# Attention over 128 heads on one core: unrolled instruction streams rewritten as loops with register addresses on four engines

## The chip, the cores and the metric

The kernel runs on one core of one Trainium2 chip. The metric is the device time of one execution in microseconds (us). A profile of one execution shows every instruction of the engines TensorE (PE, and PEld for its weight loads), VectorE (DVE), ScalarE (ACT), GpSimd (POOL) and SyncE (SP), and the DMA traffic.

## The reference

```python
B, H, Sq, Skv, Dh = 8, 16, 16, 2048, 256          # bfloat16
scale = q.shape[-1] ** -0.5
scores = jnp.einsum('bhqd,bhkd->bhqk', q, k) * scale
attn = softmax(scores, axis=-1)
return jnp.einsum('bhqk,bhkd->bhqd', attn, v)
```

There are 128 heads. Each has 16 queries, 2048 keys and 2048 values of 256 numbers. K and V are 128 MB each (2^27 bytes), read once; the queries and the output are 1 MB each.

## The kernel before, in words

The 128 heads are worked in 16 blocks of 8 heads (`G = 16`). The K of a block is two units of 4 MB, `e = 0` and `e = 1` (below: a and b), and so is its V. A unit fills one of four slots of the SBUF tensor `SL` (128 partitions x 64 rows `t` x 256 numbers, 32 KB in each partition). Two slots (`KA`, `KB`) take K and two (`VA`, `VB`) take V; block 0's K goes through the V slots and the last block's V through the K slots.

For block `g` the work is:

- SP issues all loads of K and V (line 97, in `on_sync`), each behind a wait for the work that frees its slot. The order is K a, K b of block g, then V a, V b of block g-1. The last V units are split into pieces (`TAIL_A`, `TAIL`) so that TensorE can follow them as they land. The queries come with one load into `QT` (line 100).
- VectorE turns each K unit in place with 32x32 block transposes, four instructions of 16 rows `t` for a unit (line 154).
- TensorE computes the scores into `S_ps` with 64 matmuls of 512 columns (lines 234 and 235, called by `qk`). The stationary operand is `QW`, in which ScalarE lays out the scaled queries of the block (`qwb`, line 174).
- VectorE takes the negated maximum of the scores (line 156), ScalarE the exponentials and their sums (line 206), VectorE transposes these into `PTc` (line 162) and forms the reciprocal of the sum (lines 164, 166), and ScalarE spreads `PTc` into the zero-padded stationary operand `PTz` with eight copies (line 219).
- TensorE multiplies `PTz` with V, 64 matmuls of 256 columns for a unit (line 251, `pv`), unit a into one PSUM bank and unit b into another. ScalarE scales each half of the rows into `O_fin` (`evac`, line 180) and issues the store of the block (line 184). The last block's store is issued by SP (line 133).

TensorE's blocks 1 to 15 are one loop (`nc.Fori`), with blocks 0 and the last product written out around it; the other engines' programs are fully written out. In TensorE's loop the scores of block g come first and then the product with V of block g-1. On ScalarE, block g-1's `finish` (evacuation and store) stands between block g's exponentials and block g's copies into `PTz`.

The semaphores that matter here: `s_k`, `s_v` count landed loads, `c_kt` transposed K, `c_qk` finished scores of a unit, `c_mx` the maximum, `c_ex` the exponentials, `c_pt` the transposes into `PTc`, `c_cp` the copies into `PTz`, `c_pv` finished products, `c_ev` evacuations.

Of the kernel before, what the change touches and what calls it, by code (L numbers as in the profile page):

```python
# [7 lines left out]
PE = mybir.EngineType.PE  # L8
BF16 = mybir.dt.bfloat16
F32 = mybir.dt.float32  # L10

T = 64
KA, KB, VA, VB = 0, 1, 2, 3


def bass_standalone__softmax_full_bidir__sampling_kernel(
# [17 lines left out]
    qh = q.rearrange("b h s d -> (b h) (s d)")  # L34
    oh = out.rearrange("b h s d -> (b h s) d")

    with ExitStack() as es:
# [5 lines left out]
        PTc = ec(nc.sbuf_tensor("PTc", [128, T, 32], BF16))  # L43
        PTz = ec(nc.sbuf_tensor("PTz", [128, 2, T, 128], BF16))
        O_fin = ec(nc.sbuf_tensor("O_fin", [128, 2, D], BF16))
        negm = ec(nc.sbuf_tensor("negm", [128, G], F32))
        lsum = ec(nc.sbuf_tensor("lsum", [128, G, 2], F32))
        ltot = ec(nc.sbuf_tensor("ltot", [128, G], F32))
        rinv = ec(nc.sbuf_tensor("rinv", [128, G], F32))

        S_ps = ec(nc.psum_tensor("S_ps", [128, 4, 512], F32))
        O_ps = ec(nc.psum_tensor("O_ps", [128, 4, 512], F32))
# [4 lines left out]
        s_q = sem("s_q")  # L57
        s_k = [sem("s_ka"), sem("s_kb")]
        s_k0 = [sem("s_k0a"), sem("s_k0b")]
        s_v = [sem("s_va"), sem("s_vb")]  # L60
        s_st = [sem("s_st%d" % i) for i in range(2)]
# [4 lines left out]
        c_kt = [[sem("c_kt%d%d" % (e, h)) for h in range(2)] for e in range(2)]  # L66
        c_qk = [sem("c_qka"), sem("c_qkb")]
# [5 lines left out]
        c_pv = [sem("c_pv0"), sem("c_pv1")]  # L73
        c_pl = sem("c_pl")
# [4 lines left out]
        def ap_of(t_ap, offset, dims):  # L79
            return bass.AP(tensor=t_ap.tensor, offset=offset, ap=[list(t_ap.ap[0])] + [list(d) for d in dims])  # L80


        TAIL = [(0, 19), (19, 14), (33, 10), (43, 7), (50, 5), (55, 4), (59, 3), (62, 2)]
        TAIL_A = [(0, 37), (37, 27)]
        s_tail = [sem("s_t%d" % i) for i in range(len(TAIL))]
        s_vl = [sem("s_vl%d" % i) for i in range(len(TAIL_A))]
        s_vc = sem("s_vc")
        s_kl = sem("s_kl")

        def obank(g, e):  # L90
            return e + (2 if g == last else 0)

        def kslot(g, e):
            return (VA, VB)[e] if g == 0 else (KA, KB)[e]
# [4 lines left out]
        def on_sync(eng):  # L99
            eng.dma_start(QT[:], qh).then_inc(s_q, 16)  # L100
            for e in range(2):
                load(eng, ku, 0, e, kslot(0, e), 0, T, s_k0[e])
            for g in range(1, G):
                for e in range(2):
                    if g >= 2:
                        eng.wait_ge(c_qk[e], g)
                    if (g, e) != (last, 1):
                        load(eng, ku, g, e, kslot(g, e), 0, T, s_k[e])
                    else:
                        load(eng, ku, g, e, kslot(g, e), 0, 32, s_k[e])  # L110
                        load(eng, ku, g, e, kslot(g, e), 32, 32, s_kl)
                w = g - 1
                for e in range(2):
                    if w:
                        eng.wait_ge(c_pv[e], w)
                    else:
                        eng.wait_ge(c_qk[e], 1)
                    if (w, e) != (last - 1, 1):
                        load(eng, vu, w, e, (VA, VB)[e], 0, T, s_v[e])
                        if e:  # L120
                            eng.sem_inc(s_vc, 16)
                    else:
                        load(eng, vu, w, e, VB, 0, 32, s_v[e])
                        load(eng, vu, w, e, VB, 32, 32, s_vc)

            eng.wait_ge(c_qk[0], G)
            for (a, n), s in zip(TAIL_A, s_vl):
                load(eng, vu, last, 0, KA, a, n, s)
            eng.wait_ge(c_qk[1], G)
            for (a, n), s in zip(TAIL, s_tail):  # L130
                load(eng, vu, last, 1, KB, a, n, s)
            eng.wait_ge(c_ev, 2 * last + 2)
            eng.dma_start(oh[128 * last:128 * last + 128, :], O_fin[:, last % 2, :]).then_inc(s_fin, 16)
            eng.wait_ge(s_fin, 16)

        def on_gpsimd(eng):
            eng.memset(PTz[:].rearrange("p a t c -> p (a t c)").bitcast(F32), 0.0).then_inc(c_pool, 1)  # L137

        def on_vector(eng):
            eng.memset(QW[:].rearrange("p e m x -> p (e m x)").bitcast(F32), 0.0).then_inc(c_qt, 1)  # L140
            eng.wait_ge(s_q, 16)
            qf = QT[:].bitcast(F32)
            eng.transpose(qf, qf).then_inc(c_qt, 1)  # L143
            for g in range(G):
                for e in range(2):
                    for c in range(4):
                        if g == 0 and c == 0:
                            eng.wait_ge(s_k0[e], 16)
                        elif c == 0:
                            eng.wait_ge(s_k[e], 16 * g)  # L150
                        elif (g, e, c) == (last, 1, 2):
                            eng.wait_ge(s_kl, 16)
                        x = SLf[:, kslot(g, e), 16 * c:16 * c + 16, :].rearrange("p t i -> p (t i)")
                        eng.transpose(x, x).then_inc(c_kt[e][c // 2], 1)  # L154
                eng.wait_ge(c_qk[1], g + 1)
                eng.tensor_reduce(out=negm[:, g:g + 1], in_=S_ps[:].rearrange("p c n -> p (c n)"),  # L156
                                  axis=AX.X, op=ALU.max, negate=True).then_inc(c_mx, 1)
                for h in range(2):
                    eng.wait_ge(c_ex[h], g + 1)
                    if g and h == 0:  # L160
                        eng.wait_ge(c_cp, 8 * g)
                    eng.transpose(PTc[:, 32 * h:32 * h + 32, :].rearrange("p t x -> p (t x)"),  # L162
                                  P_sb[:, 1024 * h:1024 * h + 1024]).then_inc(c_pt, 1)
                eng.tensor_reduce(out=ltot[:, g:g + 1], in_=lsum[:, g, :], axis=AX.X, op=ALU.add).then_inc(c_ri, 1)  # L164
                eng.wait_ge(c_ri, 2 * g + 1)
                eng.reciprocal(rinv[:, g:g + 1], ltot[:, g:g + 1]).then_inc(c_ri, 1)  # L166

        def on_scalar(eng):
            def qwb(g):
                Q, r = g // 4, g % 4  # L170
                for a in range(4):
                    dv = QW[32 * a:32 * a + 32, 0, 16 * a, :]
                    sv = QT[32 * Q:32 * Q + 32, :]
                    eng.activation(ap_of(dv, dv.offset, [[1024 + 512, 2], [2, 64], [1, 2]]),  # L174
                                   ap_of(sv, sv.offset + 2 * (8 * r + a), [[8, 2], [64, 64], [1, 2]]),
                                   ACTF.Copy, scale=scale).then_inc(c_qw, 1)

            def evac(g, e):
                rows = slice(64 * e, 64 * e + 64)
                eng.activation(O_fin[rows, g % 2, :], O_ps[rows, obank(g, e), 0:D],  # L180
                               ACTF.Copy, scale=rinv[rows, g:g + 1]).then_inc(c_ev, 1)

            def store(g):
                eng.dma_start(oh[128 * g:128 * g + 128, :], O_fin[:, g % 2, :]).then_inc(s_st[g % 2], 16)

            def finish(g):
                eng.wait_ge(c_ri, 2 * g + 2)
                if g >= 2:
                    eng.wait_ge(s_st[g % 2], 16 * (g // 2))
                for e in range(2):  # L190
                    eng.wait_ge(c_pv[e], g + 1)
                    evac(g, e)
                eng.wait_ge(c_ev, 2 * g + 2)
                store(g)
# [3 lines left out]
            for g in range(G):  # L198
                if g < last:
                    eng.wait_ge(c_qk[1], g + 1)  # L200
                    qwb(g + 1)
                eng.wait_ge(c_mx, g + 1)
                if g:
                    eng.wait_ge(c_pt, 2 * g)
                for h in range(2):
                    eng.activation(P_sb[:, 1024 * h:1024 * h + 1024],  # L206
                                   S_ps[:, 2 * h:2 * h + 2, :].rearrange("p c n -> p (c n)"), ACTF.Exp,
                                   bias=negm[:, g:g + 1], scale=1.0, accum_out=lsum[:, g, h:h + 1]).then_inc(c_ex[h], 1)
                if 0 < g < last:
                    finish(g - 1)  # L210
                if g == 0:
                    eng.wait_ge(c_pool, 1)
                eng.wait_ge(c_pt, 2 * g + 2)
# [104 lines left out]
```

## Time and profile before

| | |
|---|---|
| time, 3 runs | median 636.15 us, 636.04 to 636.17 |
| the profiled execution's own time | 636.1 us |
| its span, first to last instruction | 634.8 us |
| busy: PE / DVE / ACT / POOL | 77% / 58% / 34% / 1% of the span |
| granted TensorE clock, mean | 0.917 |
| moved by DMA | 270.64 MB, mean 426 GB/s |

The span is 1.3 us shorter than the time of the same execution. A row of the profile's timeline gives the start and the duration in us, then the engine, the line, the operation and what it writes and reads, then how many instructions it merges; in brackets stands how long the engine was idle before and what ended that. A row of DMA issues gives the number of loads, the KB of one, and the median us from issue to landing. A row of a table by stage gives the stretch, its length, the busy time of each engine (with the number of instructions), the granted clock, the share of time that the 16 DMA engines were busy, and GB/s.

### The profile page before, as it was taken

The numbers are of one execution on the slowest core, as the hardware profiler recorded it, in microseconds if no ns is written. First come the engines' busy times: TensorE is split into PE (matmuls) and PEld (weight loads), VectorE is DVE, ScalarE is ACT, GpSimd is POOL, SyncE is SP. The second block draws the span as 40 slices with busy tenths as digits, with TensorE's granted clock in tenths as the row PEclk, the third lists the DMA queues.
The fourth block names the chain that finished last, engine by engine and source line by source line (L and its number), as shares of the span: only waits on it lengthen the run. The fifth ranks groups of instructions, "written<-read, shape, count | busy, mean of one in ns | idle before, by whom it ended". The sixth has DMA issues, their size and how long they took to land.

```text
span 634.8 us, 6396 instructions
## 1 busy us (share of the span) xinstructions
PE 488.3 (77%) x3072; PEld 274.9 (43%) x2560; DVE 365.2 (58%) x210; ACT 214.8 (34%) x289; POOL 7.1 (1%) x5
## 2 busy tenths in 40 slices
PE   0738989595896958869597795967959689595998
PEld 0202828154271532716336262452724527144287
DVE  2968583763738546294562945739366393663830
ACT  1042252525035250342513325142252322524170
POOL 4000000000000000000000000000000000000000
PEclk9978999798997989969799797998979989798899
DMA  8999999999999999999999999999999999999997
GB/s 376 436 441 432 428 432 432 430 430 431 432 429 434 429 432 433 429 434 429 433 430 429 432 429 433 430 430 433 434 429 436 433 433 432 432 432 425 430 425 285
DMA packets 13113, 270.64 MB, mean 426 GB/s; under 512 B 1456, under 2 KB 3760, under 8 KB 4400
## 3 DMA queue, kind: packets, MB, share of 16 engines
q1 hardware_dynamic: 10944, 269.55, 98.8%
q10 hardware_dynamic: 2160, 0.98, 0.5%
q8 instruction: 3, 0.05, 0.0%
q14 instruction: 6, 0.05, 0.0%
HBM read 269.48 MB, written 1.05 MB: 426 GB/s over the span
## 4 chain that ended last, share of the span: by engine, by line
DMA 58%; PE 23%; DVE 16%; ACT 2%; issue 0%; SPq 0%
DMA SL<-in_k_dram 58%; DVE SL L154 15%; PE S_ps L234 11%; PE S_ps L235 10%; PE O_ps L251 2%; ACT PTz L219 1%; DVE PTc L162 1%; DVE negm L156 1%; ACT P_sb L206 0%; ACT O_fin L180 0%; SPq L97 0%; SPq L100 0%; DVE rinv L166 0%; DVE ltot L164 0%
## 5 line engine op out<-in xcount | busy, mean ns | idle before, releaser
L154 DVE STREAM_TRANSPOSE SL<-SL 128x2048 f32<-128x2048 f32 x128 | 284.2, 2279 | 157.9 <-DMA SL<-in_k_dram 157.9
L234 PE MATMUL S_ps<-SL,QW 128*128 128x512 bf16 x512 | 214.0, 418 | 143.5 <-DVE SL L154 143.3
L251 PE MATMUL O_ps<-SL,PTz 128*128 128x256 bf16 x2048 | 226.3, 273 | 0.9 <-ACT PTz L219 0.7
L234 PEld LDWEIGHTS S_ps<-SL,QW 128*128 128x128 bf16 x512 | 75.1, 147 | 326.6 <-issue 171.7
L251 PEld LDWEIGHTS O_ps<-SL,PTz 128*128 128x128 bf16 x2048 | 199.8, 98 | 30.9 <-issue 4.5
L235 PE MATMUL S_ps<-SL,QW 128*128 128x512 bf16 x512 | 212.5, 415 | 0.0
L219 ACT ACTIVATE PTz<-PTc 32x1024 bf16<-32x1024 bf16 x128 | 134.9, 1054 | 11.3 <-ACT O_fin L180 5.9
L174 ACT ACTIVATE QW<-QT 32x256 bf16<-32x256 bf16 x64 | 26.8, 419 | 243.3 <-PE S_ps L235 236.2
L156 DVE TENSOR_REDUCE negm<-S_ps 128x1 f32<-128x2048 f32 x16 | 36.7, 2292 | 61.4 <-PE S_ps L235 61.4
L180 ACT ACTIVATE O_fin<-O_ps,rinv 64x256 bf16<-64x256 f32 x32 | 15.0, 468 | 137.6 <-PE O_ps L251 137.5
L162 DVE STREAM_TRANSPOSE PTc<-P_sb 128x1024 bf16<-128x1024 bf16 x32 | 37.9, 1224 | 20.3 <-ACT P_sb L206 20.3
L206 ACT ACTIVATE P_sb<-S_ps,negm 128x1024 bf16<-128x1024 f32 x32 | 35.3, 1109 | 25.5 <-DVE negm L156 25.5
L137 POOL MEMSET PTz<- 128x8192 f32 x1 | 6.9, 6924 | 0.3 <-POOLq L303 0.3
L206 ACT ACTIVATION_READ_ACCUMULATOR P_sb<-S_ps,negm 128x1 f32 x32 | 6.3, 196 | 0.0
L143 DVE STREAM_TRANSPOSE QT<-QT 128x2048 f32<-128x2048 f32 x1 | 2.3, 2312 | 3.7 <-DMA QT<-in_q_dram 3.7
L166 DVE RECIPROCAL rinv<-ltot 128x1 f32<-128x1 f32 x16 | 2.6, 164 | 0.5
L164 DVE TENSOR_REDUCE ltot<-lsum 128x1 f32<-128x2 f32 x16 | 1.8, 112 | 0.0
L174 ACT ACT_TABLE_LOAD x1 | 1.3, 1283 | 0.7 <-PEq L303 0.7
L140 DVE MEMSET QW<- 128x1024 f32 x1 | 0.9, 912 | 1.0 <-PEq L303 1.0
L303 POOL MEMSET const-bfloat16-1.0<- 128x1 bf16 x1 | 0.1, 101 | 0.0
L303 POOL MEMSET const-uint8-127<- 128x1 uint8 x1 | 0.1, 101 | 0.0
L303 POOL MEMSET const-float32-0.0<- 128x1 f32 x1 | 0.1, 98 | 0.2 <-issue 0.2
(1 smaller groups left out, 0.1 us busy)
## 6 DMA issues: line engine op xcount, KB each, us to landing
SL<-in_k_dram SPq DMA_DIRECT2D x31, 4096.0 KB, 25.8
SL<-in_v_dram SPq DMA_DIRECT2D x29, 4096.0 KB, 29.1
SL<-in_k_dram SPq DMA_DIRECT2D x2, 2048.0 KB, 23.7
SL<-in_v_dram SPq DMA_DIRECT2D x2, 2048.0 KB, 29.2
SL<-in_v_dram SPq DMA_DIRECT2D x1, 2368.0 KB, 21.6
SL<-in_v_dram SPq DMA_DIRECT2D x1, 1728.0 KB, 25.4
SL<-in_v_dram SPq DMA_DIRECT2D x1, 1216.0 KB, 20.7
QT<-in_q_dram SPq DMA_DIRECT2D x1, 1024.0 KB, 4.9
```

The costliest lines, as they stand in the source:

```text
L137: eng.memset(PTz[:].rearrange("p a t c -> p (a t c)").bitcast(F32), 0.0).then_inc(c_pool, 1)
L154: eng.transpose(x, x).then_inc(c_kt[e][c // 2], 1)
L156: eng.tensor_reduce(out=negm[:, g:g + 1], in_=S_ps[:].rearrange("p c n -> p (c n)"), axis=AX.X, op=ALU.max, negate=True).then_inc(c_mx, 1)
L162: eng.transpose(PTc[:, 32 * h:32 * h + 32, :].rearrange("p t x -> p (t x)"), P_sb[:, 1024 * h:1024 * h + 1024]).then_inc(c_pt, 1)
L166: eng.reciprocal(rinv[:, g:g + 1], ltot[:, g:g + 1]).then_inc(c_ri, 1)
L174: eng.activation(ap_of(dv, dv.offset, [[1024 + 512, 2], [2, 64], [1, 2]]), ap_of(sv, sv.offset + 2 * (8 * r + a), [[8, 2], [64, 64], [1, 2]]),
L180: eng.activation(O_fin[rows, g % 2, :], O_ps[rows, obank(g, e), 0:D], ACTF.Copy, scale=rinv[rows, g:g + 1]).then_inc(c_ev, 1)
L206: eng.activation(P_sb[:, 1024 * h:1024 * h + 1024], S_ps[:, 2 * h:2 * h + 2, :].rearrange("p c n -> p (c n)"), ACTF.Exp, bias=negm[:, g:g ...
L219: eng.activation(PTz[32 * a:32 * a + 32, z, :, 64 * e + 16 * a:64 * e + 16 * a + 16], sv[:, :, 16 * (a % 2):16 * (a % 2) + 16], ACTF.Copy) ...
L234: return eng.matmul(dst, w, x, start=start, stop=stop)
L235: return eng.add_instruction(mybir.InstMatmult(name=nc.get_next_instruction_name(), engine=PE, start_tensor_calc=start, stop_tensor_calc=stop,
L251: ins = eng.matmul(O_ps[:, bank, 0:D], PTz[:, z, t, :], SL[:, slot, t, :], start=(t == 0), stop=(t == T - 1))
```

## The change: loops on SP, DVE, ACT and PE, and what moves with them

What it does, beside turning the programs into loops whose semaphore limits and addresses come from registers:

- The queries come in four loads of 256 KB, each into 32 partitions of `QT`, with a partition's row of 8 KB as before. SP issues them ahead of the K loads.
- SP's order of loads becomes K a, K b of block j, then V b of block j-2, then V a of block j-1. The last three V units (block 14's b, both of block 15) come in pieces of 3, 2 and 8, and each waits for the part of the slot that it overwrites (`c_pv` counts every 16 rows).
- VectorE transposes block 1's K unit a ahead of block 0's maximum. A unit is transposed with two instructions of 32 rows instead of four of 16. In the loop, the two units of block g+1 come behind block g's softmax, under two tests of the loop counter.
- TensorE's block 0 scores are a small loop with four matmuls in each turn, behind four matmuls on zeros that open the sums. The main loop does, in turn r: the scores of block r, the product with V b of block r-2, the product with V a of block r-1, each under a test. Both units now add into one PSUM bank, so V a waits for the evacuation `c_ev` of the block before.
- ScalarE in turn g: queries of g+1, exponentials of g, one evacuation of block g-2 (all 128 rows at once) behind the product with V b, four copies for unit b of block g-1, the store, then four copies for unit a of block g. VectorE's transposes into `PTc` of block g wait for `c_cp`, thus for the copies of unit b of block g-1.
- GpSimd adds starting values to 12 semaphores before it clears `PTz`.

The diff, cut to its core:

```diff
-KA, KB, VA, VB = 0, 1, 2, 3
+VA, VB, KA, KB = 0, 1, 2, 3
+C = 16
...
-    qh = q.rearrange("b h s d -> (b h) (s d)")
+    qh = q.rearrange("b h s d -> (b h) (s d)").rearrange("(u a) n -> a u n", a=4)
...
+        PIECES = {(last - 1, 1): [(0, 16), (16, 14), (30, 34)], (last, 0): [(0, 37), (37, 27)],
+                  (last, 1): [(0, 16), (16, 14), (30, 11), (41, 8), (49, 6), (55, 4), (59, 3), (62, 2)]}
...
         def on_sync(eng):
-            eng.dma_start(QT[:], qh).then_inc(s_q, 16)
...
+            def load_v(w, e, a, n):
+                eng.wait_ge(c_pv, 8 * w + 4 * e + (a + n + C - 1) // C)
+                load(eng, vu, w, e, VA + e, a, n, s_p[e][a] if a else s_v[e])
+            for a in range(4):
+                eng.dma_start(QT[32 * a:32 * a + 32, :], qh[a]).then_inc(s_q, 16)
+            for g, s0, s in ((0, VA, s_k0), (1, KA, s_k)):
+                for e in range(2):
+                    load(eng, ku, g, e, s0 + e, 0, T, s[e])
+            for e in range(2):
+                eng.wait_ge(c_qk, 4 * e + 4)
+                load(eng, vu, 0, e, VA + e, 0, T, s_v[e])
+            with nc.Fori(2, G, engines=[SP]) as j:
+                for e in range(2):
+                    eng.wait_ge(c_qk, 8 * j + 4 * e - 4)
+                    load(eng, ku, j, e, KA + e, 0, T, s_k[e])
+                jj = eng.to_reg(j)
+                with eng.If_ne(jj, 2):
+                    load_v(j - 2, 1, 0, T)
+                load_v(j - 1, 0, 0, T)
+            for w, e in ((last - 1, 1), (last, 0), (last, 1)):
+                for a, n in PIECES[(w, e)]:
+                    load_v(w, e, a, n)
...
         def on_vector(eng):
...
+            def kt(e, h, slot):
+                x = SLf[:, slot, 32 * h:32 * h + 32, :].rearrange("p t i -> p (t i)")
+                eng.transpose(x, x).then_inc(c_kt, 1)
...
+            eng.wait_ge(s_k[0], 16)
+            for h in range(2):
+                kt(0, h, KA)
+            with nc.Fori(0, G, engines=[DVE]) as g:
+                eng.wait_ge(c_qk, 8 * g + 8)
...
                 for h in range(2):
                     eng.wait_ge(c_ex[h], g + 1)
-                    if g and h == 0:
-                        eng.wait_ge(c_cp, 8 * g)
+                    if h == 0:
+                        eng.wait_ge(c_cp, 8 * g + 9)
...
+                eng.reciprocal(rinv[:, bass.ds(g + 2, 1)], ltot[:]).then_inc(c_ri, 1)
+                gg = eng.to_reg(g)
+                with eng.If_lt(gg, last):
+                    with eng.If_ne(gg, 0):
+                        eng.wait_ge(s_k[0], 16 * g + 16)
+                        for h in range(2):
+                            kt(0, h, KA)
+                    eng.wait_ge(s_k[1], 16 * g + 16)
+                    for h in range(2):
+                        kt(1, h, KB)
...
         def on_scalar(eng):
...
+            with nc.Fori(0, G + 1, engines=[ACT]) as g:
+                gg = eng.to_reg(g)
+                with eng.If_lt(gg, G):
+                    eng.wait_ge(c_qk, 8 * g + 8)
+                    qwb((g + 1) & 15)
+                    eng.wait_ge(c_mx, g + 1)
...
+                g2 = eng.to_reg((g + 14) & 16)
+                with eng.If_ne(g2, 0):
+                    evac(g)
+                    copies(1)
+                    eng.wait_ge(c_ev, g)
+                    eng.dma_start(oh[(g + 14) & 15], O_fin[:, g, :]).then_inc(s_st, 16)
+                with eng.If_lt(gg, G):
+                    eng.wait_ge(c_pt, 2 * g + 2)
+                    eng.wait_ge(c_pv, 8 * g + 4)
+                    copies(0)
+                with eng.If_eq(gg, 0):
+                    copies(1)
+            evac(G + 1)
...
         def on_tensor(eng):
...
+            with nc.Fori(0, 2, engines=[PE]) as e:
+                for h in range(2):
+                    with nc.Fori(0, 4, engines=[PE]) as b:
...
+            with nc.Fori(1, G + 2, engines=[PE]) as r:
+                rr = eng.to_reg(r)
+                with eng.If_lt(rr, G):
...
+                with eng.If_ne(rr, 1):
...
+                    eng.wait_ge(c_cp, 8 * r + 1)
+                    eng.wait_ge(s_v[1], 16 * (r - 1))
+                    pv(1, lambda t: lim2 if t in dict(PIECES[(last - 1, 1)]) else lim1)
+                with eng.If_lt(rr, G + 1):
+                    lim = eng.to_reg((r & 16) + 1)
+                    eng.wait_ge(c_ev, rr)
+                    eng.wait_ge(c_cp, 8 * r + 5)
+                    eng.wait_ge(s_v[0], 16 * r)
+                    pv(0, lambda t: lim)
```

More of the change, by code (lines that the diff above doesn't have):

```diff
@@ L8 @@
 PE = mybir.EngineType.PE
+ACT = mybir.EngineType.Activation
+DVE = mybir.EngineType.DVE
+SP = mybir.EngineType.SP
 BF16 = mybir.dt.bfloat16
@@ L44, in bass_standalone__softmax_full_bidir__sampling_kernel @@
         PTz = ec(nc.sbuf_tensor("PTz", [128, 2, T, 128], BF16))
[L45 to L49, printed above, removed]
+        O_fin = ec(nc.sbuf_tensor("O_fin", [128, G + 2, D], BF16))
+        negm = ec(nc.sbuf_tensor("negm", [128, 1], F32))
+        lsum = ec(nc.sbuf_tensor("lsum", [128, 2], F32))
+        ltot = ec(nc.sbuf_tensor("ltot", [128, 1], F32))
+        rinv = ec(nc.sbuf_tensor("rinv", [128, G + 2], F32))
         S_ps = ec(nc.psum_tensor("S_ps", [128, 4, 512], F32))
-        O_ps = ec(nc.psum_tensor("O_ps", [128, 4, 512], F32))
+        O_ps = ec(nc.psum_tensor("O_ps", [128, 512], F32))
         def sem(name):
@@ L65, in bass_standalone__softmax_full_bidir__sampling_kernel @@
         c_qw = sem("c_qw")
[L66 to L67 removed]
+        c_kt = sem("c_kt")
+        c_qk = sem("c_qk")
         c_mx = sem("c_mx")
@@ L134, in on_sync @@
+                jj = eng.to_reg(j)
[5 more added lines that the diff above has]
+                    load_v(w, e, a, n)
+            eng.wait_ge(c_ev, G + 1)
+            eng.dma_start(oh[last], O_fin[:, G + 1, :]).then_inc(s_fin, 16)
             eng.wait_ge(s_fin, 16)
         def on_gpsimd(eng):
+            for x, n in [(c_ev, 1), (c_ri, 2), (c_cp, 9), (c_pv, 8)] + [(x, 1) for e in range(2) for x in s_p[e].values()]:
+                eng.sem_inc(x, n)
@@ L140, in on_vector @@
             eng.memset(QW[:].rearrange("p e m x -> p (e m x)").bitcast(F32), 0.0).then_inc(c_qt, 1)
-            eng.wait_ge(s_q, 16)
+            eng.wait_ge(s_q, 64)
             qf = QT[:].bitcast(F32)
             eng.transpose(qf, qf).then_inc(c_qt, 1)
[L144 to L156, printed above, removed]
+            def kt(e, h, slot):
+                x = SLf[:, slot, 32 * h:32 * h + 32, :].rearrange("p t i -> p (t i)")
+                eng.transpose(x, x).then_inc(c_kt, 1)
+            for e in range(2):
+                eng.wait_ge(s_k0[e], 16)
+                for h in range(2):
+                    kt(e, h, VA + e)
+            eng.wait_ge(s_k[0], 16)
[3 more added lines that the diff above has]
+                eng.wait_ge(c_qk, 8 * g + 8)
+                eng.tensor_reduce(out=negm[:], in_=S_ps[:].rearrange("p c n -> p (c n)"),
                                   axis=AX.X, op=ALU.max, negate=True).then_inc(c_mx, 1)
@@ L178, in evac @@
[L178 to L194, printed above, removed]
+                    dv = QW[32 * a:32 * a + 32, :, 16 * a:16 * a + 64, :]
@@ L196, in on_scalar, with copies @@
+            def copies(e):
+                for a in range(4):
+                    rs = 32 * (2 * e + a // 2)
+                    sv = PTc[rs:rs + 32, :, :]
+                    m = 64 * e + 16 * a
+                    eng.activation(PTz[32 * a:32 * a + 32, e, :, m:m + 16],
+                                   sv[:, :, 16 * (a % 2):16 * (a % 2) + 16], ACTF.Copy).then_inc(c_cp, 1)
             eng.wait_ge(c_qt, 2)
             qwb(0)
[L198 to L213, printed above, removed]
-                z = 1 if g == last else 0
-                for e in range(2):
-                    for a in range(4):
-                        rs = 32 * (2 * e + a // 2)
-                        sv = PTc[rs:rs + 32, :, :]
-                        eng.activation(PTz[32 * a:32 * a + 32, z, :, 64 * e + 16 * a:64 * e + 16 * a + 16],
-                                       sv[:, :, 16 * (a % 2):16 * (a % 2) + 16], ACTF.Copy).then_inc(c_cp, 1)
@@ L276, in on_tensor @@
[L276 to L283 removed]
+                    for c in cs:
+                        ins = mm(S_ps[:, c, :], QW[:, e, :, bp], SLk[:, slot, c, bp // 2, bp % 2, :, :],
+                                 e == 0 and bp == 0, e == 1 and bp == 7, c == cs[0])
@@ new lines, in qk, with pv @@
+                return ins
+            def pv(e, lims):
+                for t in range(T):
+                    if t in s_p[e]:
+                        eng.wait_ge(s_p[e][t], lims(t))
+                    ins = eng.matmul(O_ps[:, 0:D], PTz[:, e, t, :], SL[:, VA + e, t, :],
+                                     start=(e == 0 and t == 0), stop=(e == 1 and t == T - 1))
+                    if t % C == C - 1:
+                        ins.then_inc(c_pv, 1)
+            eng.wait_ge(c_qw, 4)
+            for c in range(4):
+                if c == 0:
+                    eng.wait_ge(c_pool, 1)
+                mm(S_ps[:, c, :], PTz[:, 0, 0, :], PTz[:, 0, 0:4, :].rearrange("p t m -> p (t m)"), True, False, c == 0, False)
```

151 lines of the change are left out of this document (45 added, 106 removed).

## The prediction, as it went on record

> **What bounds the kernel now.** I read the page's head, DMA slices and DMA queues first, then the table by stage, since 270 MB in 635 us suggests the stream of loads.
>
> ```profile
> span 634.8 us, 6396 instructions
> ...
> GB/s 376 436 441 432 428 432 432 430 430 431 432 429 434 429 432 433 429 434 429 433 430 429 432 429 433 430 430 433 434 429 436 433 433 432 432 432 425 430 425 285
> DMA packets 13113, 270.64 MB, mean 426 GB/s; under 512 B 1456, under 2 KB 3760, under 8 KB 4400
> ...
> q8 instruction: 3, 0.05, 0.0%
> q14 instruction: 6, 0.05, 0.0%
> ```
> ```profile
> 5.00:625.00 620.00, 480.62 (x3004) 268.25 (x2493) 364.28 (x209) 212.54 (x286) 2.65 (x1) 0.91 1.00 431
> ```
>
> From 5 to 625 us the DMA engines are busy with share 1.00 at 431 GB/s (the last two columns); only the first and last slices fall off. At that rate the bytes alone take 270.64/0.431 = 628 us of the 634.8. A unit of 4.19 MB takes 9.75 us. No engine is full. So the kernel stands on its stream of loads, and only three things can move its time: when the stream begins, whether it runs dry, and what follows the last byte.
>
> The end:
>
> ```profile
> L97 SPq DMA_DIRECT2D SL<-in_v_dram x41: 327/328/6307, 29.1 to 613.0; - x41
> ```
> ```profile
> SL<-in_v_dram SPq DMA_DIRECT2D x1, 128.0 KB, 18.8
> ```
> ```profile
> 618.53 14.15 PE L251 MATMUL O_ps<-SL,PTz 128*128 128x256 bf16 x128 [0.69 <-ACT PTz L219]
> ```
> ```profile
> 632.71 0.47 ACT L180 ACTIVATE O_fin<-O_ps,rinv 64x256 bf16<-64x256 f32 x1 [6.44 <-PE O_ps L251]
> ```
> ```profile
> 633.21 0.35 SPq L133 DMA_DIRECT2D out_dram<-O_fin  x1
> ```
>
> The last piece of V is issued at 613.0 and lands 18.8 later, at 631.8. TensorE works without a pause from 618.53 to 632.68, so the chain of waits names compute at the end, but it finishes only 0.9 us behind the last byte. The last block is all but a DMA end already: there is little for a better order to win.
>
> **The change part by part.**
>
> *Queries in four loads, ahead of K.* This is the one edit in the stream itself.
>
> ```profile
> 0.74 0.38 SPq L100 DMA_DIRECT2D QT<-in_q_dram  x1
> ...
> 1.17 2.09 SPq L97 DMA_DIRECT2D SL<-in_k_dram  x4
> 5.64 2.31 DVE L143 STREAM_TRANSPOSE QT<-QT 128x2048 f32<-128x2048 f32 x1 [3.71 <-DMA QT<-in_q_dram]
> ...
> 15.34 8.89 DVE L154 STREAM_TRANSPOSE SL<-SL 128x2048 f32<-128x2048 f32 x4 [7.39 <-DMA SL<-in_k_dram]
> ```
>
> Now 1.05 MB land by 5.64, of which 2.4 us are bytes at 431 GB/s and 2.5 the way in and out; K follows without a gap (15.34 - 5.64 = 9.7, one unit). Issues are 0.43 to 0.59 us apart, and a quarter of the queries is 0.61 us of bytes, so issuing alone opens no gap. But each quarter goes into 32 partitions, and every load in this trace goes into 128. If the rate belongs to the 16 engines, the shift is 0; below 0 is excluded, the bytes are the same on engines that are full. If it belongs to the partitions, a quarter moves at 108 GB/s: 2.4 us each, 9.7 in all, a shift of +7.3. No row is nearer to either end; I take the middle factor, half the rate: 4.9 us for the queries, **+2.4 us** on everything behind.
> [...]
>
> *Does the stream run dry? The steady round.* Compute now runs in a longer loop: the transposes into PTc of block g wait for the copies of unit b of g-1, these for the evacuation, this for V b's product, this for the scores. Rows of a round before:
>
> ```profile
> 191.90 8.89 DVE L154 STREAM_TRANSPOSE SL<-SL 128x2048 f32<-128x2048 f32 x4 [10.18 <-DMA SL<-in_k_dram]
> 201.79 8.89 DVE L154 STREAM_TRANSPOSE SL<-SL 128x2048 f32<-128x2048 f32 x4 [1.00 <-DMA SL<-in_k_dram]
> 214.52 2.29 DVE L156 TENSOR_REDUCE negm<-S_ps 128x1 f32<-128x2048 f32 x1 [3.83 <-PE S_ps L235]
> 218.08 2.37 DVE L162 STREAM_TRANSPOSE PTc<-P_sb 128x1024 bf16<-128x1024 bf16 x2 [1.27 <-ACT P_sb L206]
> ...
> 220.52 0.16 DVE L166 RECIPROCAL rinv<-ltot 128x1 f32<-128x1 f32 x1
> 230.90 4.50 DVE L154 STREAM_TRANSPOSE SL<-SL 128x2048 f32<-128x2048 f32 x2 [10.22 <-DMA SL<-in_k_dram]
> ```
> ```profile
> 221.58 0.47 ACT L180 ACTIVATE O_fin<-O_ps,rinv 64x256 bf16<-64x256 f32 x1 [2.44 <-PE O_ps L251]
> ```
> ```profile
> 580.84 8.60 ACT L219 ACTIVATE PTz<-PTc 32x1024 bf16<-32x1024 bf16 x8 [0.42 <-ACT O_fin L180]
> ```
> ```profile
> 582.41 17.66 DVE L154 STREAM_TRANSPOSE SL<-SL 128x2048 f32<-128x2048 f32 x8 [10.26 <-DMA SL<-in_k_dram]
> ```
>
> From the landing of K a (191.90) to the end of the scores (214.52) are 22.6; one product with V until its evacuation 7.06 (221.58); evacuation 0.5; four copies, half of 8.60, 4.3; PTc to the reciprocal's end 2.6. Together 37.1, and the next K a lands 39.0 later (230.90): **1.9 us spare**. When compute is late it no longer waits for K b, and a round is 17.66 + 3.84 + 7.06 + 0.5 + 4.3 + 2.6 = 36.0.
>
> To this come the register instructions S. On TensorE they hide:
>
> ```profile
> 64.93 0.38 PE L235 MATMUL S_ps<-SL,QW 128*128 128x512 bf16 x1
> 65.14 2.12 PE L251 MATMUL O_ps<-SL,PTz 128*128 128x256 bf16 x18
> ```
>
> These are in its present loop, with limits from registers between the two; the gap is an ordinary 0.21. On VectorE (the reciprocal's address, two tests, a limit) and ScalarE (a limit and addresses of the evacuation) I have no row. Below: 0. Above: as long as a DMA issue each, six times 0.34 = 2.0, from this row:
>
> ```profile
> 228.99 0.34 ACTq L184 DMA_DIRECT2D out_dram<-O_fin  x1
> ```
>
> I take 1.0. With 38.1 against 39.0 the loads still set the pace, and S costs **0**. Loop ends cost nothing either: VectorE's comes with up to 8.9 us of transposes queued, TensorE's in its wait for K, SP's far ahead of need. Scores of a unit free its K slot some 12.5 us after landing, and its next load starts moving at 29.25: 14 us beyond the 2.5 on the way. V b and V a have 16 and 18.
>
> The early rounds have less, because V b of block 0 was loaded early: K3 a lands only three units behind K2 a.
>
> ```profile
> 74.79 8.90 DVE SL L154 x4
> ```
>
> Round 2 ends at 74.8 + 36 + S and K3 a lands at 104.0, so compute is some 7 + S late and gains 3 - S a round. It must be on time at K15 a, which the new order puts six units ahead of the end: 631.8 - 58.5 = 573.3. Compute reaches it at 74.8 + 13 x round, so rounds up to 38.35 (S up to 2.35) are free. The tightest place follows: V15 a overwrites V14 a, which has landed and begun to be used at 603.5 (573.3 + 18.8 + 3.8 + 7.1 + 0.5); its first piece waits for 48 of 64 matmuls, 5.3, plus 2.5 on the way: 611.3, when the stream wants it at 612.3. About 1 us spare.
>
> *Block 1's first K unit ahead of block 0's softmax.*
>
> ```profile
> 37.78 2.29 DVE L156 TENSOR_REDUCE negm<-S_ps 128x1 f32<-128x2048 f32 x1 [3.84 <-PE S_ps L235]
> ...
> 48.41 0.65 PE L234 MATMUL S_ps<-SL,QW 128*128 128x512 bf16 x1 [10.66 <-DVE SL L154]
> ...
> 56.96 8.70 SPq L97 DMA_DIRECT2D SL<-in_k_dram  x2
> ```
>
> It lands at 34.8, so the maximum moves from 37.78 to 43.7. Maximum and exponentials (4.7) then allow block 1's scores at 48.5, against 48.41 now: K2 a is still issued near 57, and the stream has bytes until 64. **0**. The loop around block 0's scores has 13 us of cover (K1 b ends at 44.5; V0 a is wanted then).
>
> *End.* Same last piece, but TensorE now follows the pieces instead of finishing a backlog: from landing to store two matmuls (0.22), a handover (0.2) and the evacuation (0.5), 0.9 against 1.4 now; register addresses give some back. Between -0.5 and 0, I take **-0.3**. Fewer evacuations, GpSimd's 12 additions (needed at 20 us, done by 9) and doubled transposes (same rows of K): 0.
>
> Sum: 634.8 + 2.4 - 0.3 = 636.9 of span; with the 1.3 around it, **638.2**. The profiled execution took 636.1, the median 636.15, so no correction.
>
> **Rivals.**
> *A, the queries cost nothing:* the 16 engines carry 32 partitions as fast as 128. 636.15 - 0.3 = **635.9**, not slower. The place is the first 8 us, the price 2.4 us, and it decides by the width under which a load slows: above 32 partitions mine holds, at 32 or below this one. For it: share 1.00 at 431 GB/s, so the engines are what is full now. Against it: no load here leaves out a partition.
> *B, compute takes over:* from S = 2.35 each us of S costs 13 us, less the 1 spare: S = 3 gives about 646, S = 4 about **659**. Against it: TensorE's gap of 0.21. For it: nothing in the trace shows a branch on VectorE.
> [...]
> *C, the rate goes with the partitions:* +7.3, **643**.
>
> **How the numbers follow.** Mine 0.53, A 0.31, B 0.11, C 0.05. The 0.2% that a measurement can tell from no change is 1.27 us: 634.9 to 637.4. Mine (with the end at its bounds and the shift 0.6 either way, 637.4 to 639.1), B and C are slower, A is the same; some of mine falls to the same, and 0.03 is left for a faster stream. Faster 0.03, same 0.32, slower 0.65. The range holds A and mine: 635.5 to 639.6.
>
> **What would show it.** Right: queries landed near 8 instead of 5.64, first K transpose near 17.8 instead of 15.34, from there 39.0 a round and a share of 1.00 to the end. Wrong: first K at 15.3 (A) or above 20 (C); K a transposes more than 39.0 apart, idle VectorE named by the copies, slices under 425 GB/s, many more instruction packets (B); or a hole in the stream near 612, where only 1 us is spare.

## The result and the profile after

The changed kernel takes 638.0 us (median of 8 runs, 637.65 to 638.74) against 636.12 (8 runs, 635.93 to 636.34): the ratio is 1.003, 95% interval 1.0019 to 1.0041. The prediction was 638.2.

The head of the page and two of its rows of the profiled execution (its own time 638.04):

```profile
span 636.2 us, 7440 instructions
...
GB/s 330 429 429 429 428 429 435 433 437 433 441 432 433 431 431 431 431 431 432 430 429 433 429 432 429 435 433 431 433 441 432 436 433 433 429 431 431 414 413 310
...
q8 instruction: 1, 0.02, 0.0%
```

The rate in the middle is what it was; the first slice fell from 376 to 330 GB/s. So look at the first microseconds: the timeline of VectorE, and of SyncE, the changed kernel.

```profile
7.70 2.31 DVE L136 STREAM_TRANSPOSE QT<-QT 128x2048 f32<-128x2048 f32 x1 [5.76 <-DMA QT<-in_q_dram]
17.33 8.77 DVE L140 STREAM_TRANSPOSE SL<-SL 128x4096 f32<-128x4096 f32 x2 [7.32 <-DMA SL<-in_k_dram]
```
```profile
0.75 1.79 SPq L103 DMA_DIRECT2D QT<-in_q_dram  x4
2.58 1.85 SPq L94 DMA_DIRECT2D SL<-in_k_dram  x4
```

Then one row of the table by stage, 3 to 6 us, for the kernel before and for the changed one (last columns: granted clock, DMA share, GB/s):

```profile
3.00:6.00 3.00, 0.00 (x0) 0.00 (x0) 0.36 (x1) 0.00 (x0) 3.00 (x1) 1.00 1.07 451
```
```profile
3.00:6.00 3.00, 0.00 (x0) 0.00 (x0) 0.00 (x0) 0.00 (x0) 3.00 (x1) 1.00 1.03 224
```

The DMA engines are as busy as ever (share 1.03 against 1.07) and move half as much (224 against 451 GB/s). The queries are ready at 7.70 instead of 5.64, the first K at 17.33 instead of 15.34: +2.0.

The steady round, VectorE and ScalarE:

```profile
340.32 8.77 DVE L140 STREAM_TRANSPOSE SL<-SL 128x4096 f32<-128x4096 f32 x2 [1.92 <-DMA SL<-in_k_dram]
350.07 8.77 DVE L140 STREAM_TRANSPOSE SL<-SL 128x4096 f32<-128x4096 f32 x2 [0.98 <-DMA SL<-in_k_dram]
362.67 2.29 DVE L152 TENSOR_REDUCE negm<-S_ps 128x1 f32<-128x2048 f32 x1 [3.83 <-PE S_ps L234]
374.68 2.37 DVE L159 STREAM_TRANSPOSE PTc<-P_sb 128x1024 bf16<-128x1024 bf16 x2 [9.71 <-ACT PTz L197]
...
379.32 8.77 DVE L140 STREAM_TRANSPOSE SL<-SL 128x4096 f32<-128x4096 f32 x2 [1.92 <-DMA SL<-in_k_dram]
```
```profile
369.87 0.47 ACT L190 ACTIVATE O_fin<-O_ps,rinv 128x256 f32 x1 [2.56 <-PE O_ps L250]
```

K a is 39.0 after K a, as before. The new wait is there in full (9.71 us ended by the copies into PTz, where it was 1.27 ended by the exponentials), yet VectorE still stands idle for 1.92 us until K lands: the loads set the pace.

The early rounds, where compute was to be late:

```profile
99.39 2.29 DVE L152 TENSOR_REDUCE negm<-S_ps 128x1 f32<-128x2048 f32 x1 [3.84 <-PE S_ps L234]
...
114.21 17.43 DVE L140 STREAM_TRANSPOSE SL<-SL 128x4096 f32<-128x4096 f32 x4
135.47 2.29 DVE L152 TENSOR_REDUCE negm<-S_ps 128x1 f32<-128x2048 f32 x1 [3.83 <-PE S_ps L234]
```

Four transposes in a row, none waiting for a load, and a round of 135.47 - 99.39 = 36.08.

The end: the source view's row of the V loads, the row of the last piece, and the last rows of ScalarE and SyncE.

```profile
L94 SPq DMA_DIRECT2D SL<-in_v_dram x42: 327/333/493, 33.2 to 620.6; - x42
```
```profile
SL<-in_v_dram SPq DMA_DIRECT2D x1, 128.0 KB, 12.9
```
```profile
634.04 0.47 ACT L190 ACTIVATE O_fin<-O_ps,rinv 128x256 bf16<-128x256 f32 x1 [10.26 <-PE O_ps L250]
```
```profile
634.54 0.35 SPq L123 DMA_DIRECT2D out_dram<-O_fin  x1
```

The last byte lands at 620.6 + 12.9 = 633.5 (before 631.8, +1.7), and the store is issued 1.0 later (before 1.4). The span grew by 1.4. The time grew by 1.9: outside the span lie 1.84 us (mean of the 8 runs) instead of 1.3. That half microsecond the prediction did not have.

### The profile page after: what moved, and what is told of

The parts are those of the page before. It is cut to its first block, busy times and chain, and to the rows that moved or that the text cites. A ratio compares the mean times of both kernels' runs of the same rounds, so it can differ in the third digit from the quotient of the medians.

```text
span 636.2 us, 7440 instructions
## 1 busy us (share of the span) xinstructions
PE 498.1 (78%) x3076; PEld 274.0 (43%) x2561; DVE 361.2 (57%) x146; ACT 209.1 (33%) x277; POOL 7.1 (1%) x5
## 3 DMA queue, kind: packets, MB, share of 16 engines
HBM read 269.48 MB, written 1.05 MB: 425 GB/s over the span
## 4 chain that ended last, share of the span: by engine, by line
DMA 49%; PE 22%; DVE 14%; issue 11%; ACT 2%; SPq 1%; ACTq 0%; DVEq 0%
DMA SL<-in_k_dram 49%; DVE SL L140 13%; PE O_ps L250 9%; PE S_ps L233 7%; PE S_ps L234 6%; ACT PTz L197 2%; DVE PTc L159 1%; ACT O_fin L190 0%; DVE negm L152 0%; DVEq L150 0%; SPq L94 0%; SPq L103 0%; ACT P_sb L210 0%; ACTq L219 0%; ACTq L190 0%
## 5 line engine op out<-in xcount | busy, mean ns | idle before, releaser
L140 DVE STREAM_TRANSPOSE SL<-SL 128x4096 f32<-128x4096 f32 x64 | 280.3, 4422 | 42.2 <-DMA SL<-in_k_dram 41.7
L233 PE MATMUL S_ps<-SL,QW 128*128 128x512 bf16 (+1 forms) x512 | 217.2, 424 | 109.9 <-DVE SL L140 100.9
L250 PE MATMUL O_ps<-SL,PTz 128*128 128x256 bf16 x2048 | 228.7, 273 | 14.1 <-ACT O_fin L190 14.1
L234 PE MATMUL S_ps<-SL,QW 128*128 128x512 bf16 (+1 forms) x512 | 215.5, 421 | 0.0
L233 PEld LDWEIGHTS S_ps<-SL,QW 128*128 128x128 bf16 (+1 forms) x512 | 75.3, 147 | 300.2 <-issue 183.8
L184 ACT ACTIVATE QW<-QT 32x256 bf16 (+1 forms) x68 | 28.6, 420 | 319.5 <-PE S_ps L234 310.3
L190 ACT ACTIVATE O_fin<-O_ps,rinv 128x256 f32 (+1 forms) x16 | 7.6, 474 | 49.1 <-PE O_ps L250 49.1
L233 PE MATMUL S_ps<-PTz 128*128 128x512 bf16 x1 | 0.6, 609 | 11.8 <-ACT QW L184 11.8
L163 DVE RECIPROCAL rinv<-ltot 128x1 f32 x16 | 2.6, 164 | 2.4 <-DVE ltot L161 0.2
L234 PE MATMUL S_ps<-PTz 128*128 128x512 bf16 x3 | 1.5, 634 | 0.0
```

The source lines that it names most:

```text
L140: eng.transpose(x, x).then_inc(c_kt, 1)
L163: eng.reciprocal(rinv[:, bass.ds(g + 2, 1)], ltot[:]).then_inc(c_ri, 1)
L184: eng.activation(dv, sv, ACTF.Copy, scale=scale).then_inc(c_qw, 1)
L190: eng.activation(O_fin[:, n, :], O_ps[:, 0:D], ACTF.Copy, scale=rinv[:, bass.ds(n, 1)]).then_inc(c_ev, 1)
L233: return eng.matmul(dst, w, x, start=start, stop=stop, skip_group_check=not check)
L234: return eng.add_instruction(mybir.InstMatmult(name=nc.get_next_instruction_name(), engine=PE, start_tensor_calc=start, stop_tensor_calc=stop,
```

## The experiments

Theory: the price is the narrow query loads, at the front of a stream of loads that is full until the end (DMA share 1.00 from 20 to 570 us, 0.99 from 600 to 632). Rivals: the number of loads, the new schedule, the loop programs. Beside these variants the kernel before took 636.03 to 636.11.

**One wide load, in the changed kernel.**

```diff
-    qh = q.rearrange("b h s d -> (b h) (s d)").rearrange("(u a) n -> a u n", a=4)
+    qh = q.rearrange("b h s d -> (b h) (s d)")
...
-            for a in range(4):
-                eng.dma_start(QT[32 * a:32 * a + 32, :], qh[a]).then_inc(s_q, 16)
+            eng.dma_start(QT[:], qh).then_inc(s_q, 16)
...
-            eng.wait_ge(s_q, 64)
+            eng.wait_ge(s_q, 16)
```

> The changed kernel with the queries in one load over 128 partitions (in natural order, so the queries reach other heads than the reference has them; the work is the same). Theory, the narrow loads are the price: queries landed near 5.6 us instead of 7.7, first K transpose near 15.3 instead of 17.33, the whole stream 2.0 us earlier: 636.0. Rival, the late start comes from the loop program on SP: first K still near 17.3, time near 638.0.

Measured 635.85 (ratio to before 0.9997, 0.9988 to 1.0006); first K at 15.31, 440 GB/s from 3 to 6 us:

```profile
15.31 8.77 DVE L139 STREAM_TRANSPOSE SL<-SL 128x4096 f32<-128x4096 f32 x2 [7.39 <-DMA SL<-in_k_dram]
```
```profile
3.00:6.00 3.00, 0.00 (x0) 0.00 (x0) 0.39 (x1) 0.00 (x0) 3.00 (x1) 1.00 1.03 440
```

The rival falls: with the wide load the whole rewrite costs nothing in time. That is a balance: its span is 0.6 us shorter than before's (634.1 against 634.7 in the mean of the runs), and 0.5 more lies outside the span.

**Narrow loads alone, in the kernel before.**

```diff
-            eng.dma_start(QT[:], qh).then_inc(s_q, 16)
+            for a in range(4):
+                eng.dma_start(QT[32 * a:32 * a + 32, :], qh[32 * a:32 * a + 32, :]).then_inc(s_q, 16)
...
-            eng.wait_ge(s_q, 16)
+            eng.wait_ge(s_q, 64)
```

> The kernel before with only its one query load replaced by four loads into 32 partitions each. Theory, narrow loads are the price: first K transpose 2.0 us later than 15.34, everything behind it 2.0 later, less what the end absorbs (last matmul 0.9 us behind the last byte, but its chain also starts 2 later, so nothing is absorbed): 638.1. Rival, the price belongs to the new schedule: 636.1.

Measured 637.89 (1.0029, 1.0018 to 1.0039); first K at 17.30, 219 GB/s:

```profile
17.30 8.89 DVE L155 STREAM_TRANSPOSE SL<-SL 128x2048 f32<-128x2048 f32 x4 [7.35 <-DMA SL<-in_k_dram]
```
```profile
3.00:6.00 3.00, 0.00 (x0) 0.00 (x0) 0.00 (x0) 0.00 (x0) 3.00 (x1) 1.00 1.03 219
```

The edit alone makes the whole difference, in the other direction too.

**Why are they slow: width, number, or place?** Three variants in the kernel before, one in the changed one. The lines that set VectorE's wait to the number of loads are left out.

```diff
-            eng.dma_start(QT[:], qh).then_inc(s_q, 16)
+            for a in range(2):      # two of 64 partitions
+                eng.dma_start(QT[64 * a:64 * a + 64, :], qh[64 * a:64 * a + 64, :]).then_inc(s_q, 16)
+            for a in range(8):      # or eight of 16
+                eng.dma_start(QT[16 * a:16 * a + 16, :], qh[16 * a:16 * a + 16, :]).then_inc(s_q, 16)
+            for a in range(4):      # or every fourth partition
+                eng.dma_start(QT[a::4, :], qh[a::4, :]).then_inc(s_q, 16)
+            for a in range(4):      # or a quarter of the columns (changed kernel)
+                eng.dma_start(QT[:, 1024 * a:1024 * a + 1024], qh[:, 1024 * a:1024 * a + 1024]).then_inc(s_q, 16)
```

> The kernel before with its query load in two loads of 64 partitions each (rows of 8 KB as before). Theory, a range of 64 partitions moves at half the full rate just as one of 32 does: queries 2.0 us late again, first K near 17.3, time 638.0. Rival, the price goes with the number of loads (four loads 2.0, so two a third of the three extra: 0.7): first K near 16.0, time 636.8. Rival, the rate goes with the partitions up to the engines' 431 GB/s: 64 at full rate, 636.1.

> The kernel before with its query load in eight loads of 16 partitions in a row. [...] Rival, the price goes with the number of loads, 0.65 us for each after the first: 4.6 us, first K near 20, time near 640.6. Rival, half the rate is the floor: 2.0 to 2.5 late, 638.3.

> The kernel before with its query load in four loads of 32 partitions, but every fourth partition instead of 32 in a row (rows of 8 KB, same bytes, same number of loads). [...] Rival, the number of loads or of partitions makes the price: first K near 17.3, time 637.9.

> The changed kernel with the queries still in four loads of 256 KB, but each over 128 partitions and a quarter of the columns (rows of 2 KB, natural order, so queries reach other heads). Theory, the price lies in the 32 partitions: first K near 15.4, time near 636.1. Rival, four loads cost by being four (issues, the way in and out of each): first K near 17.3, time near 638.0.

| queries in | GB/s, 3 to 6 us | first K at | time | ratio to before |
|---|---|---|---|---|
| 1 load of 128 partitions (before) | 451 | 15.34 | 636.1 | |
| 2 of 64 in a row | 229 | 17.49 | 638.21 | 1.0034 (1.002 to 1.0047) |
| 4 of 32 in a row (before's loop) | 219 | 17.30 | 637.89 | 1.0029 (1.0018 to 1.0039) |
| 8 of 16 in a row | 126 (3 to 8 us) | 20.41 | 641.25 | 1.0083 (1.0065 to 1.0101) |
| 4 of 32, every fourth | 279 | 18.47 | 638.49 | 1.0039 (1.0027 to 1.0051) |
| 4 of 128, a quarter of the row (changed kernel) | 265 | 17.79 | 637.3 | 1.002 (1.0011 to 1.0029) |

The rows of the table by stage for 2 of 64, 8 of 16, and every fourth:

```profile
3.00:6.00 3.00, 0.00 (x0) 0.00 (x0) 0.00 (x0) 0.00 (x0) 3.00 (x1) 1.00 1.04 229
```
```profile
3.00:8.00 5.00, 0.00 (x0) 0.00 (x0) 0.00 (x0) 0.00 (x0) 4.65 (x1) 1.00 1.01 126
```
```profile
3.00:6.00 3.00, 0.00 (x0) 0.00 (x0) 0.00 (x0) 0.00 (x0) 3.00 (x1) 1.00 0.84 279
```

The DMA share is 1.04 and 1.01 in the first two: the engines are occupied, not unfed. Two loads cost as much as four (638.21 against 637.89), which refutes the count; 64 partitions in a row (229 GB/s) move no faster than 32 (219), and 16 (126) at somewhat over half of that, so the loss is not in proportion to the width either. The eight loads taken by themselves did not decide: the first K came 5.1 us late, where the rival by the number of loads had 4.6 and a quarter of the 431 GB/s, my estimate, would give 7 (1.05 MB in 9.7 us instead of 2.4); 126 GB/s is more than that quarter.

The last two lines of the table do not follow. If a range in a row were the whole reason, every fourth partition would move at the full rate, with the first K near 15.4; I had expected that, and the rival by number of loads or of partitions had 17.3. It moved 279 GB/s, with the first K at 18.47, later than either (its seven runs lie between 637.56 and 639.70, wider apart than any other's). So a range in a row is not the whole reason. Loads over all 128 partitions with 2 KB rows were slow too (265 GB/s), with the first K 2.5 us behind the wide load's 15.31; the third K unit is still 2.5 behind (37.22 against 34.75), and the time is 1.45 behind its 635.85. Rows, number of loads and choice of partitions are mixed in these two, and what slows them stays open. What is shown is that the form of the query loads makes the difference; why a form is slow is not.

**Narrow loads beside K, on ScalarE's queue,** without the last wait (next).

```diff
         def on_sync(eng):
...
-            for a in range(4):
-                eng.dma_start(QT[32 * a:32 * a + 32, :], qh[a]).then_inc(s_q, 16)
...
         def on_scalar(eng):
...
+            for a in range(4):
+                eng.dma_start(QT[32 * a:32 * a + 32, :], qh[a]).then_inc(s_q, 16)
             eng.wait_ge(c_qt, 2)
...
-            eng.wait_ge(s_fin, 16)
```

> The changed kernel with its four narrow query loads issued by ScalarE's queue instead of SP's, so that the K loads run beside them, and without TensorE's last wait. [...] Rival, an engine that is held up by a narrow load holds up its K packets too: K0 b near 27, time 637.5.

Measured 643.02 (1.0113, 1.0095 to 1.0131), worse than either. A stage of it, the row of its query loads, and VectorE's first wait:

```profile
2.00:26.00 24.00, 0.00 (x0) 0.00 (x0) 1.35 (x1) 1.28 (x1) 6.60 (x1) 1.00 0.96 317
```
```profile
QT<-in_q_dram ACTq DMA_DIRECT2D x4, 256.0 KB, 15.3
```
```profile
24.65 2.31 DVE L134 STREAM_TRANSPOSE QT<-QT 128x2048 f32<-128x2048 f32 x1 [22.71 <-DMA QT<-in_q_dram]
```

From 2 to 26 us the engines have share 0.96 and move 317 GB/s, where the changed kernel moves 392: busy engines move less, which fits narrow loads that hold up the K packets; how they would is not shown. The queries land only at 24.65 instead of 7.70. VectorE's transposes of block 0's K stand behind that of the queries, so block 0 starts late as well:

```profile
68.57 7.38 SPq L94 DMA_DIRECT2D SL<-in_k_dram  x2
```

This load, K2 a, is issued at 68.57 instead of 59.84, and from 60 to 80 us the stream moves 392 GB/s. An estimate from these rates and the changed kernel's (392 from 2 to 26, and 443 from 60 to 80): 24 x (392 - 317) / 431 = 4.2 us for the first stretch and 20 x (443 - 392) / 431 = 2.4 for the second, 6.6 together, where the time is 5.5 above 637.53 (the same kernel with the loads on SP, next). With 224 GB/s beside the wide load's 451 I had expected K to fill what the narrow loads leave, and a time of 635.5; that fell. The rival (an engine that is held up holds up its K packets, 637.5) had the sign and too small a price.

**TensorE's last wait.**

```diff
-            eng.wait_ge(s_fin, 16)      # on TensorE, behind its loop
```

> The changed kernel without TensorE's last instruction, the wait for the last store's landing. The profiled execution's time is 1.84 us longer than its span here and 1.3 before. Theory, this wait keeps TensorE's end behind the last store and adds the 0.5 outside the span: time 637.5 at the same span of 636.2. Rival, the 0.5 comes from another part of the programs (loops, registers): time stays 638.0.

Measured 637.53 (1.0023, 1.0014 to 1.0033), the theory's number; but these runs (637.29 to 637.78) overlap those of the changed kernel (637.65 to 638.74), so the time alone does not give the size. The time above the span says more: in the ten runs it is 1.56 us in the mean, against 1.84 with the wait, so 0.3 of the 0.5 is outside the span as expected and 0.2 is a shorter span, which the theory did not explain. The other variants here that keep the wait have 1.67 to 1.82, and the two others without it (the one above and the last one below) 1.3, as before. The wait costs 0.3 to 0.5 us.

**Block 1's first K unit back behind block 0's softmax.**

```diff
-            eng.wait_ge(s_k[0], 16)
-            for h in range(2):
-                kt(0, h, KA)
...
-                    with eng.If_ne(gg, 0):
-                        eng.wait_ge(s_k[0], 16 * g + 16)
-                        for h in range(2):
-                            kt(0, h, KA)
+                    eng.wait_ge(s_k[0], 16 * g + 16)
+                    for h in range(2):
+                        kt(0, h, KA)
```

> The changed kernel with block 1's first K unit transposed behind block 0's softmax again (one wait and two transposes moved into the loop). Theory: block 1's scores of the first unit start near 54.5 (transposes from 46) instead of near 50.5, K2 a is issued some 2 us later than 59.84, and the stream has bytes until 66: no change, 638.0. Rival: the early transpose keeps the stream fed in the first rounds; without it a hole opens before K2 a and the time rises by 1 us or more.

Measured 639.21 (1.0048, 1.0035 to 1.0062): 1.2 more than the changed kernel (its lowest run, 638.99, is above the highest of the changed kernel, 638.74), so the early transposes are worth something and my 0 was wrong. VectorE without them, the load it delays, and the stage behind (of a profiled execution that took 639.95, the longest of the five):

```profile
44.99 2.29 DVE L149 TENSOR_REDUCE negm<-S_ps 128x1 f32<-128x2048 f32 x1 [9.09 <-PE S_ps L230]
```
```profile
65.91 7.38 SPq L94 DMA_DIRECT2D SL<-in_k_dram  x2
```
```profile
64.00:72.00 8.00, 8.00 (x38) 2.64 (x19) 4.83 (x2) 0.00 (x0) 0.00 (x0) 1.00 0.78 303
```

VectorE waits 9.09 us for block 0's scores, where it was 3.84 in the kernel before; K2 a is issued at 65.91 (59.84 in the changed kernel), when the stream has run out, and from 64 to 72 us it moves 303 GB/s (436 in the changed kernel). Why the scores are late is read from TensorE's rows of the changed kernel, where block 0's scores are a small loop; no run here writes that loop out:

```profile
36.73 0.44 PE L233 MATMUL S_ps<-SL,QW 128*128 x1 [0.33 <-issue]
37.01 0.39 PE L234 MATMUL S_ps<-SL,QW 128*128 x1
37.23 0.38 PE L233 MATMUL S_ps<-SL,QW 128*128 x1
37.45 0.38 PE L234 MATMUL S_ps<-SL,QW 128*128 x1
38.11 0.44 PE L233 MATMUL S_ps<-SL,QW 128*128 x1 [0.28 <-issue]
```

A turn of four matmuls takes 1.4 us where four written out, 0.22 apart as within a turn, take 0.88. Block 0 has 16 such turns, and its scores end about 5 us late. In the changed kernel the early transposes (36.75 to 45.5) fill just that time.

**Spare of the round.** One and three more transposes of 1024 columns on VectorE in every turn.

```diff
                 eng.reciprocal(rinv[:, bass.ds(g + 2, 1)], ltot[:]).then_inc(c_ri, 1)
+                for h in range(1):        # 3 in the second
+                    eng.transpose(PTx[:, h, :], P_sb[:, 0:1024])
```

> The changed kernel with one more transpose of 1024 columns (1.2 us, its result unused) on VectorE in every turn behind the reciprocal. A late round takes 36.08 us in the changed kernel (maximum 99.39 to 135.47), so 37.3 with it, under the 38.25 at which compute reaches the last K in time (77.06 + 13 rounds = 574.35). Theory: 638.0. Rival, the spare is used up already: 638 + 13 x 1.2 = 653.

> The same with three such transposes (3.7 us): a round of 39.75, over the 38.25. Theory: compute takes over, the last K is transposed 13 x 1.5 = 19.5 us late, one of it spare: 656.5. Rival, the loads' queue absorbs it, having 14 us of loads ahead: 638 to 642.

One: 637.91 (1.0027, 1.0016 to 1.0038), free; a late round is 37.01 (maximum 99.22 to 136.23). Three: 651.34 (1.0237, 1.0221 to 1.0253), where 656.5 was forecast. Its last rounds on VectorE, and two stages:

```profile
570.27 2.29 DVE L153 TENSOR_REDUCE negm<-S_ps 128x1 f32<-128x2048 f32 x1 [3.84 <-PE S_ps L237]
...
588.31 17.38 DVE L141 STREAM_TRANSPOSE SL<-SL 128x4096 f32<-128x4096 f32 x4
609.53 2.29 DVE L153 TENSOR_REDUCE negm<-S_ps 128x1 f32<-128x2048 f32 x1 [3.83 <-PE S_ps L237]
```
```profile
500.00:570.00 70.00, 53.55 (x319) 27.77 (x253) 48.83 (x23) 20.74 (x25) 0.00 (x0) 0.88 1.00 426
...
600.00:610.00 10.00, 10.00 (x50) 3.57 (x28) 6.17 (x3) 0.24 (x1) 0.00 (x0) 1.00 0.41 177
```

A round is 39.26, not the 39.75 expected: three transposes take 3.48 instead of 3.7, and the round grew by only 3.2 (36.08 to 39.26); what covers the other 0.3 is not shown. The last K a is transposed at 588.31, 13.96 behind the changed kernel's 574.35, and the time rose by 13.3. With the measured round the rule gives 13 x (39.26 - 38.25) = 13.1. Until 570 us the stream shows nothing (share 1.00); the lateness is paid all at once near 600, where it empties.

**A version under both.** One wide load, the order of the queries set right on chip, no last wait.

```diff
...
+            def spread(Q):
+                for a in range(4):
+                    eng.activation(QTd[32 * a:32 * a + 32, Q, :, :, :], QTs[32 * Q:32 * Q + 32, a, :, :, :],
+                                   ACTF.Copy).then_inc(c_q2, 1)
             eng.wait_ge(c_qt, 2)
+            spread(0)
+            eng.wait_ge(c_q2, 4)
             qwb(0)
+            for Q in range(1, 4):
+                spread(Q)
+            eng.wait_ge(c_q2, 16)
...
-            eng.wait_ge(s_fin, 16)
```

> The changed kernel with its queries in one load over 128 partitions in natural order, 16 copies on ScalarE at the start that bring them into the order that the loop's addresses want (four ahead of block 0's queries, 12 behind), and without TensorE's last wait. Theory: the wide load gives back 2.0, the last wait 0.5, ScalarE's 16 copies of about 1.05 us end near 27 us, ahead of block 0's scores, so cost nothing: 635.4, under the kernel before (636.04) by 0.6. Rival: the copies delay block 0 and drain the stream of loads, over 636.

Measured 635.35 against 636.11: ratio 0.999, 0.9981 to 0.9999. The gain is a tenth of a percent, just clear of none: all 11 runs (635.24 to 635.78) lie under all 18 of before (635.88 to 636.22). ScalarE's start shows the copies done at 28.06, 15 us before it is wanted:

```profile
8.02 4.47 ACT L205 ACTIVATE QT<-QT 32x1024 bf16<-32x1024 bf16 x4 [6.00 <-DVE QT L137]
12.52 1.74 ACT L187 ACTIVATE QW<-QT 32x256 bf16<-32x256 bf16 x4
14.28 13.78 ACT L205 ACTIVATE QT<-QT 32x1024 bf16<-32x1024 bf16 x12
43.19 1.74 ACT L187 ACTIVATE QW<-QT 32x256 bf16 x4 [15.13 <-PE S_ps L247]
```

## Why the prediction was right, point by point

- **The stream is the bound.** Shown: undoing the query loads alone brings the changed kernel back to before, and making them narrow alone brings before to the changed kernel's time; one more transpose on VectorE in every round costs nothing (637.91).
- **Queries, +2.4.** Right in kind, 0.4 too large: +2.0 at the first K, +1.7 at the last byte. Half the rate was a middle taken between two ends, which no row of the trace before chose; that 224 GB/s confirm it is luck as far as the rows go. Rivals A (635.9) and C (643) fall.
- **The round.** 36.0 + S was forecast; 36.08 was measured, of which the transposes as two instructions instead of four gave back 0.2 (17.43 against 17.66), so S is about 0.3, not 1.0. The edge at 38.35 and the price of 13 us for each us beyond it are borne out: a round of 37.01 is free, one of 39.26 costs 13.3. No run lies between the two, so the edge is bracketed and not measured. Rival B did not come about: it needs an S above 2.35. Instruction packets, one sign named for it, fell from 9 to 1, and no run here shows what such a packet costs. Another sign did show, two slices under 425 GB/s near the end (414 and 413); but with the wide load they are 421 and 416 at a time of 635.85, so late compute is not what they mean.
- **The tightest place, V15 a near 612.** No hole: share 0.99 from 600 to 620. The rate there is 407 GB/s, against 424 before; why full engines move less there is not shown.
- **Block 1's first K unit, 0.** Wrong for the edit alone: it is worth 1.2 us here, because it fills the time in which block 0's scores are late. I had weighed that loop only against the next V load, with 13 us of cover, and not against K2 a, which stands two steps later on the path with about 6. Made together, the two edits come to the forecast 0.
- **The end, -0.3.** From last byte to store 1.4 became 1.0: right.
- **Around the span.** Taken as 1.3, was 1.84: missing from the sum, 0.3 to 0.5 of it TensorE's last wait. It balances what the queries were overrated by, so part of the closeness of 638.2 to 638.0 is luck.

## What to carry to other kernels

Where the loads are the bound, look for what keeps the DMA engines busy at a lower rate: here 1 MB of queries in four narrow loads instead of one wide one, at the head of the stream (224 GB/s at share 1.03), was the whole loss (638.0 against 635.85). A longer chain of waits was free at a round of 37.01 us (637.91) and cost 13.3 us at 39.26 (651.34), and the edge between the two, 38.35, could be added up from rows; beyond it the stream hid the lateness until the end here (share 1.00 until 600 us, 0.41 from 600 to 610), so the middle of the profile did not show it. Cost an edit together with the ones that cover it, and count what lies behind the span too (1.84 us here against 1.3).

## What the runs showed that I had not expected

- The narrow loads did more harm beside other traffic than ahead of it: 643.02 with the queries on a second queue, 637.53 with them in front. Part of it is block 0, which waits for the queries.
- 32 partitions spread over the whole range (279 GB/s) and 128 partitions in rows of 2 KB (265) were only a fifth to a quarter faster than 32 in a row (219 to 224), and the first K behind them came later (18.47 and 17.79 against 17.30).
- Block 0's loop of four matmuls on TensorE costs about 0.5 us a turn (1.4 us, where four at 0.22, as within a turn, take 0.88); the large loop's 0.21 us between scores and products told nothing of that.
- TensorE's wait at the very end, with no work behind it, was not free: 0.3 to 0.5 us of time (637.53 without it against 638.0; 1.56 against 1.84 us outside the span).
